# Window attention followed by four experts: reordered loads, junk matmuls in batch 0, and interleaved expert layers

## The chip, the cores and the metric

The kernel runs on one core of a Trainium2 chip. The metric is the device time of one execution, in microseconds (us). Most figures below are medians of several runs. Every run here was of the ordinary, fast state. A profile is one such execution, taken by the hardware profiler; its span is about 1.7 us shorter than the time measured for the same execution.

The array's granted clock is either full or half (1.0 or 0.5) in every record. The first record starts at 42.5 us in the profile before, and for the time before it the profile prints 1.00. Start-to-start distances of matmuls tell the truth there: matmuls of 512 columns at recorded half clock start 0.43 us apart, at full clock 0.22.

## The reference, cut to what matters

```
scores = (q @ k.T) / 8              # 4 batches, 8 heads, 768 positions, 64 wide
keep   = key < 4  or  0 <= query - key < 128
a      = softmax(where(keep, scores, -1e9))
x      = (a @ v), heads side by side          # 3072 tokens x 512
p      = domain_probs / sum(domain_probs)
out    = sum over 4 experts of p[:, e] * (relu(x @ w1[e]) @ w2[e])   # 512 -> 1024 -> 512
```

## The kernel before

Attention goes by batch (four) and by pair of heads (four per batch). A pair transposes q and k on TensorE (trq, trk), copies them out, multiplies scores (spsum), takes exp on ScalarE, multiplies by the mask on VectorE, multiplies by V (opsum), normalises, and transposes back (trx) into xT. This is a serial chain. The names ending in psum, and trq, trk and trx, are buffers in PSUM, the memory that the kernel's matmuls write to. Reading such a buffer out, for hpsum by the relu, is called its eviction; in these programs the next matmuls into it come after that. The experts take tokens in chunks of 512: 8 groups of 4 matmuls (hpsum), relu, then 4 groups of 8 matmuls (mopsum).

The order in the program text is not the order on the engine; it is laid out at compile time. The program has the experts behind all of attention, yet in the trace before an hpsum matmul starts at 32.89 us, within batch 0. So expert matmuls stand among attention's, and in these traces a matmul that waits holds up those behind it (one of them for 2.22 us, below).

The parts that the change touches, cut:

```
# 1. GpSimd builds the masks, then issues every load
nc.gpsimd.memset(MASK, 1.0) ... nc.gpsimd.affine_select(...) x 13
nc.gpsimd.dma_start(out=dp_nat, ...)
# 2. loads of a pair stand inside the pair: 4 for q and k, 2 for v
for hp in range(NHP):
    for ph in range(2): nc.gpsimd.dma_start(out=qn[:, :, ph, :], ...); (same for kn)
    ...
# 3. order of the whole
emit_attention_batch(0); emit_weight_loads(0); emit_weight_loads(1)
emit_attention_batch(1); emit_weight_loads(2); emit_weight_loads(3)
emit_attention_batch(2); emit_attention_batch(3)
# 4. experts
for c in range(NCH):
    for e in range(E):
        for fb in range(NFB):        # 8 groups of 4 hpsum matmuls, two PSUM buffers
            ...; relu -> ht
        for sub in range(NSUB):      # 4 groups of 8 mopsum matmuls
            ...
    nc.sync.dma_start(out=<1 MB of the chunk>, in_=out_sb)
```

The softmax here doesn't subtract the row's maximum and nothing guards it: scores larger than these inputs give would overflow.

Of the kernel before, what the change touches and what calls it, by code (L numbers as in the profile page):

```python
# [9 lines left out]
ALU = mybir.AluOpType  # L10
AX = mybir.AxisListType
FP32 = mybir.dt.float32
BF16 = mybir.dt.bfloat16
# [3 lines left out]
def kernel(  # L17
# [12 lines left out]
    nc = tc.nc  # L30

    B, H, S, D = q.shape
    NSINK = int(n_sink)
    WIN = int(window)
    E, Dm, F = moe_w1.shape
# [28 lines left out]
    def out_contribs(qb):  # L64
# [24 lines left out]
    ps_h = ctx.enter_context(tc.tile_pool(name="ps_h", bufs=2, space=bass.MemoryType.PSUM))  # L89
    ps_o = ctx.enter_context(tc.tile_pool(name="ps_o", bufs=2, space=bass.MemoryType.PSUM))  # L90

    ident = consts.tile([P, P], BF16, name="ident")
    nc.gpsimd.memset(ident, 1.0)
    nc.gpsimd.affine_select(
        out=ident, in_=ident, compare_op=ALU.is_ge, fill=0.0,
        base=0, pattern=[[1, P]], channel_multiplier=-1,
    )
    nc.gpsimd.affine_select(
        out=ident, in_=ident, compare_op=ALU.is_ge, fill=0.0,
        base=0, pattern=[[-1, P]], channel_multiplier=1,  # L100
    )

    MASK = consts.tile([P, AT_W], BF16, name="MASK")
    nc.gpsimd.memset(MASK, 1.0)  # L104

    def sel_diag(cs):
        nc.gpsimd.affine_select(  # L107
            out=MASK[:, cs : cs + P], in_=MASK[:, cs : cs + P],
            compare_op=ALU.is_ge, fill=0.0,
            base=0, pattern=[[1, P]], channel_multiplier=-1,  # L110
        )

    def sel_prev(cs):
        nc.gpsimd.affine_select(  # L114
            out=MASK[:, cs : cs + P], in_=MASK[:, cs : cs + P],
            compare_op=ALU.is_gt, fill=0.0,
            base=0, pattern=[[-1, P]], channel_multiplier=1,
        )

    sel_diag(0)  # L120
    sel_prev(P)
    nc.gpsimd.memset(MASK[:, 2 * P : S], 0.0)
    nc.gpsimd.memset(MASK[0:NSINK, 0:S], 1.0)
    for jb in range(1, NJB):
        cs = JB_ACOL[jb]
        sel_diag(cs)
        if jb < NJB - 1:
            sel_prev(cs + P)

    dp_nat = consts.tile([P, Ntok // P, E], FP32, name="dp_nat")  # L130
    nc.gpsimd.dma_start(  # L131
        out=dp_nat, in_=moe_domain_probs.rearrange("(tb p) e -> p tb e", p=P)
    )
    rowsum = consts.tile([P, Ntok // P], FP32, name="rowsum")
    nc.vector.reduce_sum(out=rowsum, in_=dp_nat, axis=AX.X)
    recip_rs = consts.tile([P, Ntok // P], FP32, name="recip_rs")
    nc.vector.reciprocal(out=recip_rs, in_=rowsum)
    scale_t = consts.tile([P, Ntok // P, E], FP32, name="scale_t")
    nc.vector.tensor_mul(
        scale_t, dp_nat, recip_rs[:, :, None].to_broadcast([P, Ntok // P, E])  # L140
    )

    w1_sb = {}
    w2_sb = {}

    def emit_weight_loads(e):
        for db in range(NDB):
            t = wpool.tile([P, F], BF16, name=f"w1_{e}_{db}", tag=f"w1_{e}_{db}")
            nc.gpsimd.dma_start(out=t, in_=moe_w1[e, db * P : (db + 1) * P, :])
            w1_sb[(e, db)] = t  # L150
        for fb in range(NFB):
            t = wpool.tile([P, Dout], BF16, name=f"w2_{e}_{fb}", tag=f"w2_{e}_{fb}")
            nc.gpsimd.dma_start(out=t, in_=moe_w2[e, fb * P : (fb + 1) * P, :])  # L153
            w2_sb[(e, fb)] = t

    xT = []
    for hp in range(NHP):
        t = xtp.tile([P, Ntok], BF16, name=f"xT_{hp}", tag=f"xT_{hp}")
        xT.append(t)

    def emit_attention_batch(b):
        for hp in range(NHP):
            h0 = 2 * hp
            qn = ap_sb.tile([P, NQB, 2, D], BF16, name="qn", tag="qknat", bufs=8)
            kn = ap_sb.tile([P, NQB, 2, D], BF16, name="kn", tag="qknat", bufs=8)
            for ph in range(2):
                nc.gpsimd.dma_start(  # L167
                    out=qn[:, :, ph, :],
                    in_=q[b, h0 + ph].rearrange("(sb p) d -> p sb d", p=P),
                )  # L170
                nc.gpsimd.dma_start(  # L171
                    out=kn[:, :, ph, :],
                    in_=k[b, h0 + ph].rearrange("(sb p) d -> p sb d", p=P),
                )
            qT = ap_sb.tile([P, S], BF16, name="qT", tag="qkT", bufs=8)
            kT = ap_sb.tile([P, S], BF16, name="kT", tag="qkT", bufs=8)
            trq = ps_mix.tile([P, S], BF16, name="trq", tag="mix")
# [8 lines left out]
            nc.scalar.copy(out=qT, in_=trq)  # L186
            nc.vector.tensor_copy(out=kT, in_=trk)  # L187

            vx = []
            for ph in range(2):  # L190
                vext = ap_sb.tile([P, NJB, 72], BF16, name="vext", tag="vext", bufs=8)
                nc.gpsimd.dma_start(  # L192
                    out=vext[:, :, 0:D],
                    in_=v[b, h0 + ph].rearrange("(jb p) d -> p jb d", p=P),
                )
                nc.gpsimd.memset(vext[:, :, D : D + 1], 1.0)
                vx.append(vext)

            onat = ap_sb.tile([P, NQB, P], BF16, name="onat", tag="onat", bufs=4)

            for ph in range(2):
                pb = ph * 64
                aT = ap_sb.tile([P, AT_W], BF16, name="aT", tag="aT", bufs=4)
                for (cstart, cwidth, mms) in CHUNKS:
                    spsum = ps_mix.tile([P, cwidth], FP32, name="spsum", tag="mix")
                    off = 0
                    for (jb, qoff, ncols) in mms:
                        qs = JB_QSTART[jb] + qoff
                        nc.tensor.matmul(  # L209
                            spsum[:, off : off + ncols],  # L210
                            lhsT=kT[pb : pb + 64, jb * P : (jb + 1) * P],
                            rhs=qT[pb : pb + 64, qs : qs + ncols],
                            start=True,
                            stop=True,
                        )
                        off += ncols
                    nc.scalar.activation(  # L217
                        out=aT[:, cstart : cstart + cwidth],
                        in_=spsum[:, 0:cwidth],
                        func=AF.Exp,  # L220
                        scale=scale,
                    )
                    nc.vector.tensor_mul(  # L223
                        aT[:, cstart : cstart + cwidth],
                        aT[:, cstart : cstart + cwidth],
                        MASK[:, cstart : cstart + cwidth],
                    )

                opsum = ps_aout.tile([P, NQB, 66], FP32, name="opsum", tag="ao")
                for qb in range(NQB):  # L230
                    contribs = out_contribs(qb)
                    for ci, (jb, acol) in enumerate(contribs):
                        nc.tensor.matmul(  # L233
                            opsum[:, qb, 0 : D + 1],
                            lhsT=aT[:, acol : acol + P],
                            rhs=vx[ph][:, jb, 0 : D + 1],
                            start=(ci == 0),
                            stop=(ci == len(contribs) - 1),
                        )
# [5 lines left out]
                    recip[:, :, None].to_broadcast([P, NQB, D]),  # L245
                )

            trx = ps_mix.tile([P, S], BF16, name="trx", tag="mix")
            for qb in range(NQB):
                nc.tensor.transpose(  # L250
# [1 line left out]
                )  # L252
            nc.vector.tensor_copy(out=xT[hp][:, b * S : (b + 1) * S], in_=trx)

    emit_attention_batch(0)
    emit_weight_loads(0)
    emit_weight_loads(1)
    emit_attention_batch(1)
    emit_weight_loads(2)
    emit_weight_loads(3)  # L260
    emit_attention_batch(2)
    emit_attention_batch(3)

    relu_ct = 0
    for c in range(NCH):
        t0 = c * CH
        out_sb = mo_sb.tile([P, NSUB, Dout], FP32, name="out_sb", tag="osb", bufs=2)
        for e in range(E):
            hts = []
            for fb in range(NFB):  # L270
                hpsum = ps_h.tile([P, CH], FP32, name="hpsum", tag="h")
                for db in range(NDB):
# [4 lines left out]
                        start=(db == 0),  # L277
                        stop=(db == NDB - 1),
                    )
                ht = mo_sb.tile([P, CH], BF16, name="ht", tag="hT", bufs=18)  # L280
                relu_ct += 1
                if relu_ct % 3 == 0:
                    nc.vector.tensor_scalar_max(out=ht, in0=hpsum, scalar1=0.0)  # L283
                else:
                    nc.scalar.activation(out=ht, in_=hpsum, func=AF.Relu)  # L285
                hts.append(ht)
            for sub in range(NSUB):
                tb = c * NSUB + sub
                dst = out_sb[:, sub, :]
                opsum = ps_o.tile([P, Dout], FP32, name="mopsum", tag="o")  # L290
                for fb in range(NFB):
                    nc.tensor.matmul(  # L292
                        opsum,
                        lhsT=hts[fb][:, sub * P : (sub + 1) * P],
                        rhs=w2_sb[(e, fb)],
                        start=(fb == 0),
                        stop=(fb == NFB - 1),
                    )
                sc = scale_t[:, tb, e : e + 1]
                if e == 0:  # L300
                    nc.vector.tensor_scalar(  # L301
                        out=dst, in0=opsum, scalar1=sc, scalar2=None, op0=ALU.mult
                    )
                else:
                    nc.vector.scalar_tensor_tensor(  # L305
                        out=dst,
                        in0=opsum,
                        scalar=sc,
                        in1=dst,
                        op0=ALU.mult,  # L310
                        op1=ALU.add,
                    )
        nc.sync.dma_start(
            out=out[t0 : t0 + CH, :].rearrange("(s p) d -> p s d", p=P),
            in_=out_sb,
        )


# [33 lines left out]
```

## Time and profile before

| | before |
|---|---|
| time, median of 16 runs | 462.99 us (460.71 to 465.5) |
| span of the profile | 460.7 us |
| first transpose on TensorE | 14.99 us |
| first pair of batch 1 begins | 59.16 us |
| last matmul ends | 454.63 us |

The page of the kernel before: the busy time of each engine (PE is TensorE's matmuls, PEld its weight loads, DVE VectorE, ACT ScalarE, POOL GpSimd), then two rows of the span in 40 slices (busy tenths of TensorE, and its granted clock in tenths of full speed).

```profile
PE 429.9 (93%) x2528; PEld 207.0 (45%) x2528; DVE 202.3 (44%) x387; ACT 154.0 (33%) x273; POOL 113.8 (25%) x198
...
PE   0568899999999999999999999999999999999994
...
PEclk9999559999999999999999999999999999999999
```

TensorE is at least 90% busy from the sixth slice to the last but one. One slice is 11.5 us, and the two slices marked 5 ran at half clock, so the loose part is the first 70 us. The slices before them are marked 9 because no clock change was recorded before 42.5 us.

The timeline of TensorE in the kernel before: start us, length us, line, operation, out<-in, count, and in brackets the idle time before it and what ended it.

```profile
14.99 0.69 PE L180 MATMUL trq<-ident,qn 128*128 128x128 bf16 x5 [14.99 <-DMA qn<-in_q_dram]
...
26.05 0.31 PE L180 MATMUL trq<-ident,qn 128*128 128x128 bf16 x1
26.16 0.31 PE L183 MATMUL trk<-ident,kn 128*128 128x128 bf16 x1
...
32.89 0.61 PE L273 MATMUL hpsum<-xT,w 128*128 128x512 bf16 x1 [2.22 <-DMA w<-in_moe_w_dram]
```

Three things are to be read here. TensorE did nothing for 15 us. Transposes of 128 columns start 0.107 us apart, as they do later where half clock is recorded (46 to 70 us); they start 0.056 us apart after 72 us, at recorded full clock. And an expert matmul, placed early, held the queue for 2.22 us until its weights landed.

Why 15 us: the timeline of GpSimd (POOL), which issues the loads.

```profile
6.75 0.28 POOL L107 TENSOR_SCALAR_AFFINE_SELECT MASK<-MASK 128x128 bf16<-128x128 bf16 x1
6.99 1.55 POOL L131 DMA_DIRECT2D dp_nat<-in_moe_domain_probs_dram  x1
8.54 0.83 POOL L167 DMA_DIRECT2D qn<-in_q_dram  x1
```

The first load of q is issued only at 8.54 us, behind the masks and a small load that nobody needs yet.

Busy time by stretch. The first four stretches are the four pairs of batch 0, the fifth is the first pair of batch 1. Columns: the stretch and its length, busy us (and instructions) of PE, PEld, DVE, ACT and POOL, then granted clock, DMA share and GB/s.

```profile
15.00:25.80 10.80, 8.38 (x62) 4.96 (x63) 4.89 (x13) 5.04 (x9) 10.80 (x18) 1.00 1.87 119
25.80:39.00 13.20, 9.32 (x67) 5.40 (x65) 5.58 (x14) 4.93 (x9) 9.39 (x19) 1.00 1.40 168
39.00:48.60 9.60, 7.79 (x67) 4.95 (x66) 5.45 (x14) 4.62 (x9) 6.09 (x12) 0.86 1.17 204
48.60:59.20 10.60, 9.09 (x67) 5.26 (x66) 5.45 (x14) 5.04 (x9) 9.87 (x15) 0.50 1.77 147
...
59.10:72.50 13.40, 13.40 (x83) 6.29 (x81) 6.09 (x15) 7.12 (x13) 13.40 (x25) 0.60 1.77 116
```

A warning about the busy column. TensorE is shown busy for 8.38 of 10.8 us in the first pair, but it is slow, not full: at the distances seen at full clock (0.056 us for a transpose, 0.029 for an output matmul, 0.22 for 512 columns) the same matmuls would need less than half of that (an estimate).

The chain of waits in the dense part: start us, length us, what.

```profile
300.64 7.11 PE hpsum L273 x32
307.75 6.91 PE mopsum L292 x32
314.65 7.07 PE hpsum L273 x32
```

32 matmuls of the first layer take 0.16 to 0.20 us more than 32 of the second. Start to start, the last matmul of an hpsum group takes 241 ns on average and all others 215 to 216. After 90 late group ends (219 ns and more, from 200 us on) the next matmul starts 50 to 54 ns after a relu has ended: it waits for the eviction.

### The profile page before, as it was taken

What the parts mean: (1) busy time and instruction counts of PE and PEld (TensorE: products, weight loads), DVE (VectorE), ACT (ScalarE), POOL (GpSimd) and SP (SyncE); (2) the same over time, 40 slices, a digit from 0 to 9 for tenths busy, and PEclk for the clock granted to TensorE, in tenths of its full rate; (3) what the DMA queues carried; (4) which work ended last, traced back from release to release, by engine and by line L of the source; (5) the groups of instructions that cost most, each with busy time, mean ns of one, the idle gap of its engine ahead of it and who ended that gap; (6) DMA issues with size and microseconds to landing.
All of it is one profiled execution on the core that took longest, in us unless ns stands there. A gap on an engine that the chain in (4) does not pass through costs nothing.

```text
span 460.7 us, 6303 instructions
## 1 busy us (share of the span) xinstructions
PE 429.9 (93%) x2528; PEld 207.0 (45%) x2528; DVE 202.3 (44%) x387; ACT 154.0 (33%) x273; POOL 113.8 (25%) x198
## 2 busy tenths in 40 slices
PE   0568899999999999999999999999999999999994
PEld 0344545555555554444444444444444444444441
DVE  0345546867767773333332333233333323333332
ACT  1435455476566752211223211222211232212220
POOL 9985896699940000000000000000000000000000
PEclk9999559999999999999999999999999999999999
DMA  1999999999990002000020000200001000200002
GB/s 7 127 143 204 162 119 172 205 129 119 117 61 1 2 1 91 1 0 0 1 91 1 1 0 1 91 1 1 1 38 53 1 0 1 90 1 1 1 1 91
DMA packets 85437, 24.58 MB, mean 53 GB/s; under 512 B 76144, under 2 KB 80288, under 8 KB 85408
## 3 DMA queue, kind: packets, MB, share of 16 engines
q0 software_dynamic: 82240, 17.88, 43.4%
q1 hardware_dynamic: 3168, 6.29, 3.6%
q8 instruction: 20, 0.33, 0.3%
q14 instruction: 9, 0.07, 0.0%
HBM read 35.70 MB, written 6.29 MB: 91 GB/s over the span
## 4 chain that ended last, share of the span: by engine, by line
PE 90%; POOL 6%; DVE 1%; DMA 1%; issue 0%; ACT 0%; POOLq 0%
PE hpsum L273 38%; PE mopsum L292 37%; PE spsum L209 7%; PE opsum L233 4%; POOL kn L171 1%; PE trx L250 1%; POOL qn L167 1%; POOL vext L192 1%; PE trq L180 1%; PE trk L183 1%; DMA w<-in_moe_w_dram 1%; DVE onat L242 1%; POOL MASK L104 0%; POOL dp_nat L131 0%; POOL MASK L107 0%; POOL MASK L114 0%
## 5 line engine op out<-in xcount | busy, mean ns | idle before, releaser
L273 PE MATMUL hpsum<-xT,w 128*128 128x512 bf16 x768 | 185.8, 383 | 2.2 <-DMA w<-in_moe_w_dram 2.2
L292 PE MATMUL mopsum<-w,ht 128*128 128x512 bf16 x768 | 178.2, 380 | 0.0
L285 ACT ACTIVATE ht<-hpsum 128x512 bf16<-128x512 f32 x128 | 76.5, 597 | 223.0 <-PE hpsum L273 223.0
L273 PEld LDWEIGHTS <-w 128*128 128x128 bf16 x768 | 73.5, 97 | 96.3 <-issue 21.4
L292 PEld LDWEIGHTS <-ht 128*128 128x128 bf16 x768 | 74.0, 98 | 88.5 <-issue 5.7
L305 DVE SCALAR_TENSOR_TENSOR out_sb<-mopsum,scale_t,out_sb 128x512 f32<-128x512 f32 x72 | 54.0, 750 | 74.9 <-PE mopsum L292 74.9
L283 DVE TENSOR_SCALAR ht<-hpsum 128x512 bf16<-128x512 f32 x64 | 44.2, 691 | 87.0 <-PE hpsum L273 86.1
L217 ACT ACTIVATE aT<-spsum 128x512 bf16<-128x512 f32 (+1 forms) x128 | 65.3, 576 | 17.0 <-PE spsum L209 16.3
L223 DVE TENSOR_TENSOR aT<-aT,MASK 128x512 bf16<-128x512 bf16 (+1 forms) x128 | 49.3, 402 | 22.7 <-ACT aT L217 19.9
L209 PE MATMUL spsum<-qT,kT 64*128 64x256 bf16 (+2 forms) x224 | 47.3, 318 | 1.7 <-ACT qT L186 1.6
L233 PEld LDWEIGHTS <-aT 128*128 128x128 bf16 x480 | 25.3, 105 | 17.9 <-DVE aT L223 4.3
L233 PE MATMUL opsum<-vext,aT 128*128 128x65 bf16 x480 | 31.2, 206 | 2.2 <-DVE onat L242 2.0
L186 ACT COPY qT<-trq 128x768 bf16<-128x768 bf16 x16 | 12.8, 799 | 52.8 <-PE trq L180 40.9
L171 POOL DMA_DIRECT2D kn<-in_k_dram x32 | 30.1, 941 | 0.7 <-PE trk L183 0.7
L167 POOL DMA_DIRECT2D qn<-in_q_dram x32 | 29.8, 931 | 1.5 <-PE trk L183 0.8
L192 POOL DMA_DIRECT2D vext<-in_v_dram x32 | 28.9, 948 | 4.3 <-issue 2.7
L180 PE MATMUL trq<-ident,qn 128*128 128x128 bf16 x96 | 15.1, 247 | 15.0 <-DMA qn<-in_q_dram 15.0
L301 DVE TENSOR_SCALAR out_sb<-mopsum,scale_t 128x512 f32<-128x512 f32 x24 | 18.0, 750 | 23.7 <-PE mopsum L292 23.7
L209 PEld LDWEIGHTS <-kT 64*128 64x128 bf16 x224 | 18.3, 101 | 21.6 <-DVE kT L187 9.0
L153 POOL DMA_DIRECT2D w<-in_moe_w_dram x32 | 17.5, 588 | 13.4 <-DMA w<-in_moe_w_dram 12.6
L242 DVE TENSOR_TENSOR onat<-opsum,recip 128x384 bf16<-128x384 f32 x32 | 17.7, 554 | 0.5
L180 PEld LDWEIGHTS <-qn 128*128 128x128 bf16 x96 | 10.6, 113 | 15.0 <-issue 15.0
(26 smaller groups left out, 94.2 us busy)
## 6 DMA issues: line engine op xcount, KB each, us to landing
out_dram<-out_sb SPq DMA_DIRECT2D x6, 1024.0 KB, 4.3
w<-in_moe_w_dram POOLq DMA_DIRECT2D x16, 256.0 KB, 6.3
w<-in_moe_w_dram POOLq DMA_DIRECT2D x32, 128.0 KB, 7.3
qn<-in_q_dram POOLq DMA_DIRECT2D x32, 96.0 KB, 3.8
kn<-in_k_dram POOLq DMA_DIRECT2D x32, 96.0 KB, 3.8
vext<-in_v_dram POOLq DMA_DIRECT2D x32, 96.0 KB, 3.6
dp_nat<-in_moe_domain_probs_dram POOLq DMA_DIRECT2D x1, 48.0 KB, 5.5
```

Source lines behind the costliest of these rows:

```text
L167: nc.gpsimd.dma_start(out=qn[:, :, ph, :], in_=q[b, h0 + ph].rearrange("(sb p) d -> p sb d", p=P),)
L171: nc.gpsimd.dma_start(out=kn[:, :, ph, :], in_=k[b, h0 + ph].rearrange("(sb p) d -> p sb d", p=P),)
L192: nc.gpsimd.dma_start(out=vext[:, :, 0:D], in_=v[b, h0 + ph].rearrange("(jb p) d -> p jb d", p=P),)
L209: nc.tensor.matmul(spsum[:, off : off + ncols], lhsT=kT[pb : pb + 64, jb * P : (jb + 1) * P], rhs=qT[pb : pb + 64, qs : qs + ncols], start ...
L217: nc.scalar.activation(out=aT[:, cstart : cstart + cwidth], in_=spsum[:, 0:cwidth], func=AF.Exp, scale=scale,)
L223: nc.vector.tensor_mul(aT[:, cstart : cstart + cwidth], aT[:, cstart : cstart + cwidth], MASK[:, cstart : cstart + cwidth],)
L233: nc.tensor.matmul(opsum[:, qb, 0 : D + 1], lhsT=aT[:, acol : acol + P], rhs=vx[ph][:, jb, 0 : D + 1], start=(ci == 0), stop=(ci == len(co ...
L273: nc.tensor.matmul(hpsum, lhsT=w1_sb[(e, db)][:, fb * P : (fb + 1) * P], rhs=xT[db][:, t0 : t0 + CH], start=(db == 0), stop=(db == NDB - 1),)
L283: nc.vector.tensor_scalar_max(out=ht, in0=hpsum, scalar1=0.0)
L285: nc.scalar.activation(out=ht, in_=hpsum, func=AF.Relu)
L292: nc.tensor.matmul(opsum, lhsT=hts[fb][:, sub * P : (sub + 1) * P], rhs=w2_sb[(e, fb)], start=(fb == 0), stop=(fb == NFB - 1),)
L305: nc.vector.scalar_tensor_tensor(out=dst, in0=opsum, scalar=sc, in1=dst, op0=ALU.mult, op1=ALU.add,)
```

## The change

Its intent: start the chain of batch 0 sooner, keep the array at full clock through it with matmuls whose result is thrown away ("junk"), and hide the eviction of hpsum. The core of the diff:

```diff
+    junk = consts.tile([P, 512], BF16, name="junk")
+    nc.vector.memset(junk, 0.25)
+    junk_ps = ps_o.tile([P, 512], FP32, name="junk_ps", tag="o")
+    def warm(lhsT, rhs, n): ...            # n matmuls into junk_ps
+    warm(junk[:, 0:P], junk, 18)           # at the start
-    nc.gpsimd.dma_start(out=dp_nat, ...)
+    nc.sync.dma_start(out=dp_nat, ...)
     ...
+    first_loads[(0, 0)] = emit_loads(0, 0) # first pair's loads, then the masks
+    ident, MASK: memsets now on nc.vector, affine_selects on nc.gpsimd
     ...
     def emit_attention_batch(b):
         for hp in range(NHP):
+            if b == 0 and hp == 2: emit_w1_load(0)
             ...                            # V of both heads in one load
+            if b == 0:
+                for cs in (0, 512, 1024):
+                    for t in aTs:
+                        warm(t[:, cs : cs + P], t[:, cs : cs + 512], 2)
     ...
     emit_attention_batch(0)
     emit_weight_loads(0)                   # w2 of an expert in one load
+    first_loads[(1, 0)] = emit_loads(1, 0); first_loads[(1, 1)] = emit_loads(1, 1)
     emit_weight_loads(1)                   # (the same for batch 2)
     ...
+                (ht has 20 buffers instead of 18)
                 hts.append(ht)
+                if fb % 2 == 1 and pending_mm2:
+                    pending_mm2.pop(0)()   # second layer of the expert before
             for sub in range(NSUB):
+                pending_mm2.append(make_mm2(c, e, sub, hts, out_sb))
-        nc.sync.dma_start(out=<1 MB of the chunk>, in_=out_sb)
+                (inside make_mm2, e == 3)   nc.sync.dma_start(out=<256 KB of sub>, in_=dst)
```

## The prediction

> **What bounds it now.** TensorE. From 72 us to the end its matmuls are back to back (stretches table: 10.0 of 10 us busy). One 512-column matmul every 216 ns is the floor there; only the last matmul of each hpsum group takes 239 ns, 192 times (4.5 us in all), which I read as a wait for one of the two hpsum buffers to be evicted. So nothing is gained on VectorE, ScalarE or GpSimd as such; the time to win is before 72 us and after the last matmul (454.6 us; span 460.7).
>
> The front, from the timeline: GpSimd first builds the masks (to 7.0 us) and issues dp_nat (to 8.5), so the first transpose waits until 15.0. The four head pairs of batch 0 then take 10.7, 13.1 (2.2 of it an hpsum matmul that waits for a weight DMA), 9.7 and 10.6 us, to 59.2. Within a pair there is a serial chain: transposes, copies, scores, exp, mask, output, normalise, transpose. TensorE is also slow there: transposes start 107 ns apart, against 56 ns after 72 us; output matmuls about 55 against 29. [...]granted clock 0.50 from 50 to 70 us, full after; the 1.0 recorded before 40 us contradicts the 107 ns and is not to be believed.
>
> **The change.** (a) Loads first, masks later, merged V and w2 issues. GpSimd starts at 0.8 us; the second qn issue ends near 3.2, and before it took 4.0 us from there to the first transpose: about 7.2 instead of 15.0. Gain 7.8. (b) 18 junk matmuls fill the wait for that load ([...]free), and 12 per pair (2.6 us warm, 10.4 in all) fill gaps of batch 0, to keep the clock. A warm pair, estimated from the partly warm third pair (9.7) less the cold transposes and the cold last output group, is 8.3 us of chain with 3.6 of TensorE work; junk fits mostly, costing perhaps 0.7. So four pairs take 36 us: batch 0 ends near 43 instead of 59.2. (c) 59 to 70 us, now at half clock, becomes warm: 5.4 us. (d) Interleaving second-layer matmuls with the first-layer ones hides the hpsum eviction: up to 4.5, say 3. (e) The final store is 256 KB instead of 1 MB: 1 to 2 us off the tail. Weights and batch 1 loads should land before they are needed; GpSimd issues less.
>
> **Sum.** Batch 0 to 43.3; then 1528 expert matmuls x 216.4 ns = 330.7; 12 pairs at 4.55 us (what the dense region before paid, switching included) = 54.6; leftover waits 1.5; tail 4.3: span 434.4. Median was 2.2 over the span: **437 us**, range 429 to 446. Faster by over 2%: 0.95; within: 0.04; slower: 0.01.
>
> **What would show it.** First real transpose at 7 to 8 us; transposes of batch 0 56 ns apart; its pairs 8.5 to 9.5 us each; batch 1 begins at 41 to 46; no clock near 0.5 after 8 us; hpsum group ends at 216 ns; TensorE dense from batch 1 on; last matmul to end about 4.3 us.
>
> **What would make it wrong.** The compile-time order puts junk or hpsum matmuls ahead of chain work, and TensorE, in order, waits behind them; junk is too thin and the clock falls back (pairs 10.6 us, total 444); the 16-byte dp_nat packets delay the first q and k; weights late after batch 0; the next pair's transposes overlap the chain (better: 430).

## The result, and the profile after

| | before | after |
|---|---|---|
| time, median | 462.99 us (16 runs) | 438.12 us (11 runs, 436.21 to 439.52) |
| span of the profile | 460.7 | 437.4 |
| first transpose | 14.99 | 7.93 |
| the four pairs of batch 0, start to start | 10.9, 13.2, 9.6, 10.6 | 8.5, 12.4, 8.5, 8.5 |
| batch 1 begins | 59.16 | 45.77 |
| last matmul ends | 454.63 | 433.21 |
| from there to the end | 6.04 | 4.17 |

The ratio of the times is 0.9463 (95% interval 0.9439 to 0.9487). Ratios here are the mean time of one kernel's fast runs over that of the other's of the same rounds, so they are not quite the ratios of the quoted medians. A twelfth run of the changed kernel, of 440.89 us, is not counted there; with it the median would be 438.15.

The page of the kernel after:

```profile
PE 427.1 (98%) x2594; PEld 206.9 (47%) x2594; DVE 206.1 (47%) x392; ACT 152.8 (35%) x273; POOL 85.5 (20%) x133
...
PE   7899999999999999999999999999999999999996
...
PEclk9979999999999999999999999999999999999999
```

The empty front is gone. One slice is still marked with a reduced clock, the third (22 to 33 us).

TensorE's timeline after:

```profile
1.52 6.57 PE L100 MATMUL junk_ps<-junk 128*128 128x512 bf16 x18 [1.52 <-DVE junk L95]
7.93 0.22 PE L172 MATMUL trq<-ident,qn 128*128 128x128 bf16 x1
7.98 0.22 PE L175 MATMUL trk<-ident,kn 128*128 128x128 bf16 x1
...
18.64 0.60 PE L348 MATMUL hpsum<-xT,w 128*128 128x512 bf16 x2 [1.40 <-DMA w<-in_moe_w_dram]
```

The transposes start 0.05 to 0.06 us apart from the first on. But an hpsum matmul waits for weights again, in the second pair. The stretches after, again four pairs of batch 0 and the first of batch 1:

```profile
7.90:16.40 8.50, 7.28 (x75) 4.40 (x74) 5.02 (x13) 4.82 (x9) 8.50 (x17) 1.00 1.21 84
16.40:28.80 12.40, 10.75 (x80) 5.33 (x77) 5.59 (x14) 4.93 (x9) 10.59 (x15) 0.72 1.90 166
28.80:37.30 8.50, 7.85 (x81) 4.53 (x78) 5.58 (x14) 4.82 (x9) 4.80 (x7) 1.00 1.70 169
37.30:45.80 8.50, 7.85 (x80) 4.53 (x78) 5.58 (x14) 4.81 (x9) 6.83 (x11) 1.00 2.08 174
...
45.70:54.90 9.20, 8.94 (x86) 4.87 (x84) 6.05 (x15) 6.82 (x13) 4.57 (x7) 1.00 1.26 183
```

The second pair stands out: 12.4 us at a mean clock of 0.72. The first pair of batch 1, with 83 matmuls in 13.4 us before, now has 86 in 9.2 us, at a mean granted clock of 1.00 instead of 0.60.

The chain of waits in the dense part after:

```profile
300.25 1.73 PE mopsum L316 x8
301.98 1.73 PE hpsum L348 x8
303.71 1.73 PE mopsum L316 x8
```

Eight matmuls of either layer now take the same time; every one starts 216 ns after the one before.

The span fell by 23.3 us. Along the time axis that is 13.4 to the start of batch 1 (59.16 to 45.77), 8.0 from there to the last matmul (395.5 to 387.4), and 1.9 after it.

### The profile page after: what moved, and what is told of

It reads as the page before. It is cut to its first block, busy times and chain, and to the rows that moved or that the text cites. A ratio compares the mean times of both kernels' runs of the same rounds, so it can differ in the third digit from the quotient of the medians.

```text
span 437.4 us, 6407 instructions
## 1 busy us (share of the span) xinstructions
PE 427.1 (98%) x2594; PEld 206.9 (47%) x2594; DVE 206.1 (47%) x392; ACT 152.8 (35%) x273; POOL 85.5 (20%) x133
## 4 chain that ended last, share of the span: by engine, by line
PE 93%; POOL 3%; DMA 1%; ACT 1%; DVE 0%; issue 0%; POOLq 0%
PE mopsum L316 39%; PE hpsum L348 38%; PE spsum L193 7%; PE opsum L217 3%; PE junk_ps L100 2%; DMA w<-in_moe_w_dram 1%; PE trx L239 1%; PE trq L172 1%; PE trk L175 1%; POOL qn L141 1%; POOL kn L145 1%; ACT qT L178 1%; POOL vx L150 0%; ACT aT L201 0%; POOL MASK L260 0%
## 5 line engine op out<-in xcount | busy, mean ns | idle before, releaser
L348 PE MATMUL hpsum<-xT,w 128*128 128x512 bf16 x768 | 190.1, 379 | 1.4 <-DMA w<-in_moe_w_dram 1.4
L316 PE MATMUL mopsum<-w,ht 128*128 128x512 bf16 x768 | 187.7, 379 | 0.0
L193 PE MATMUL spsum<-qT,kT 64*128 64x256 bf16 (+2 forms) x224 | 41.0, 284 | 2.7 <-ACT qT L178 1.6
L141 POOL DMA_DIRECT2D qn<-in_q_dram x32 | 27.3, 854 | 20.4 <-DMA w<-in_moe_w_dram 19.0
L217 PEld LDWEIGHTS <-aT 128*128 128x128 bf16 x480 | 24.9, 99 | 13.3 <-DVE aT L207 2.3
L217 PE MATMUL opsum<-vx,aT 128*128 128x65 bf16 x480 | 28.7, 196 | 0.4
L145 POOL DMA_DIRECT2D kn<-in_k_dram x32 | 27.2, 851 | 3.0 <-PE opsum L217 1.4
L150 POOL DMA_DIRECT2D vx<-in_v_dram x16 | 16.6, 1041 | 2.8 <-DMA w<-in_moe_w_dram 2.7
L100 PE MATMUL junk_ps<-aT 128*128 128x512 bf16 x48 | 15.2, 416 | 0.0
L172 PE MATMUL trq<-ident,qn 128*128 128x128 bf16 x96 | 12.4, 219 | 0.0
L175 PE MATMUL trk<-ident,kn 128*128 128x128 bf16 x96 | 12.4, 219 | 0.0
```

The costliest lines, as they stand in the source:

```text
L100: nc.tensor.matmul(junk_ps[:, 0 : rhs.shape[-1]], lhsT=lhsT, rhs=rhs, start=True, stop=True,)
L141: nc.gpsimd.dma_start(out=qn[:, :, ph, :], in_=q[b, h0 + ph].rearrange("(sb p) d -> p sb d", p=P),)
L145: nc.gpsimd.dma_start(out=kn[:, :, ph, :], in_=k[b, h0 + ph].rearrange("(sb p) d -> p sb d", p=P),)
L193: nc.tensor.matmul(spsum[:, off : off + ncols], lhsT=kT[pb : pb + 64, jb * P : (jb + 1) * P], rhs=qT[pb : pb + 64, qs : qs + ncols], start ...
L217: nc.tensor.matmul(opsum[:, qb, 0 : D + 1], lhsT=aT[:, acol : acol + P], rhs=vx[:, ph, jb, 0 : D + 1], start=(ci == 0), stop=(ci == len(co ...
L316: nc.tensor.matmul(opsum, lhsT=hts[fb][:, sub * P : (sub + 1) * P], rhs=w2_sb[e][:, fb, :], start=(fb == 0), stop=(fb == NFB - 1),)
```

## The experiments

All results were correct. Each run timed its kernel beside the kernel before on the same chip. For comparison with the changed kernel I give the median, and the ratio to the kernel before where a difference is small. The starting theory was that the gain is the sum of four things: earlier loads, full clock, hidden eviction, short last store. The main rival was that the junk is mere filler, since batch 0 is a serial chain over other engines.

### Without any junk

```diff
-    warm(junk[:, 0:P], junk, 18)        (and junk, junk_ps)
-            if b == 0: ... warm(t[...], t[...], 2)
```

> After the change, with both kinds of junk matmuls taken out and nothing else. Clock theory: without them the array stays at half clock through batch 0 (transposes 107 ns apart, pairs near 10.6 us instead of 8.5) and some 10 us into batch 1, as before the change; batch 1 begins near 50 to 52 us instead of 45.8, and the time is 446 to 450 us (438.1 with junk). Rival, early loads alone: batch 0 is bound by a serial chain over ScalarE and VectorE, the junk is filler, and the time stays 436 to 439.

Measured: 446.8 us. The pairs took 11.1, 9.6, 9.6 and 10.6 us and batch 1 began at 47.9 us. Its first pair:

```profile
47.80:61.20 13.40, 13.40 (x84) 6.33 (x83) 6.09 (x15) 7.14 (x13) 8.01 (x13) 0.60 1.86 178
```

So the junk is worth 8.7 us between medians, and the rival falls. But the time was not where I expected most of it. In the profiles batch 0 ends only 2.1 us later without junk; another 4.2 us is lost in the first pair of batch 1 (13.4 us against 9.2), at a mean clock of 0.60 against 1.00. Together these are the 6.3 us between the two profiles; the profiled run was the fastest of the four without junk. That batch 0 loses so little is partly because the changed kernel has a bad second pair of its own: against a later variant without that fault (a_fill below, batch 1 at 43.1 us) batch 0 ends 4.8 us later.

### Only the start burst, and only the junk in the pairs

```diff
a_startonly:  -  if b == 0: ... warm(t[...], t[...], 2)
a_pairsonly:  -  warm(junk[:, 0:P], junk, 18)
```

> After the change with the 18 junk matmuls at the start kept and the 12 per pair taken out. Clock theory: the first pair runs at full clock (8.5 us or less), but TensorE is only busy about 40% within a pair, so the clock falls back in the second pair and stays low until batch 1: 444 to 448 us. Rival, the start burst alone is enough: 436 to 439.

> After the change with the 18 junk matmuls at the start taken out and the 12 per pair kept. Clock theory: the first pair begins at half clock (107 ns transposes) and its own junk, twice as long then, delays it, so it takes 11 to 12 us; the junk releases the clock by the second pair. Cost 2 to 4 us against the changed kernel: 440 to 442. If the per-pair junk is worth nothing: near the kernel without any junk.

Measured: 445.3 us with the start burst alone, as expected, and 439.1 with the pair junk alone, less than the 440 to 442 expected. The clock of the burst was lost during the first pair (recorded fall at 14.2 us). The junk in the pairs does nearly all of the work. With pair junk alone the first pair took 13.3 us instead of 8.5, and the first transpose could start at 6.95 us, a microsecond earlier than behind the burst. TensorE's timeline shows that only this one could:

```profile
6.95 0.27 PE L169 MATMUL trq<-ident,qn 128*128 128x128 bf16 x1 [6.95 <-POOL MASK L264]
7.69 0.27 PE L172 MATMUL trk<-ident,kn 128*128 128x128 bf16 x1 [0.47 <-DMA kn<-in_k_dram]
```

The second one waits for k, and the twelfth starts at 8.71 us, against 8.54 behind the burst. Yet batch 1 began at 45.69 us, as in the changed kernel (45.77): there the second pair gives back what the burst won. The ratios are 0.9514 and 0.9463 with overlapping intervals, so the worth of the burst, 1 us between medians and 2.4 by the ratios, is not resolved.

### Without interleaving, and interleaving alone

```diff
a_nointer:  -                if fb % 2 == 1 and pending_mm2: pending_mm2.pop(0)()
            -                pending_mm2.append(make_mm2(...))
            +                make_mm2(c, e, sub, hts, out_sb)()
b_inter:    the kernel before, with the interleaved expert loop (1 MB stores kept)
```

> After the change with the second-layer matmuls of an expert put back straight behind its first-layer ones. Buffer theory: the last matmul of each hpsum group takes 239 ns again instead of 216 in the dense part, about 23 ns for some 160 to 190 groups, so 4 to 5 us more: 442 to 443. Rival, interleaving did nothing: 438.

> The kernel before with only the interleaving of second-layer matmuls added (1 MB stores kept). Buffer theory: last matmuls of hpsum groups 216 instead of 241 ns in the dense part, 25 ns x 192 = 4.8 us at most: 458 to 459 us against 462.9. The kernel after without interleaving lost 8.8, of which its group ends at 255 ns explain about 7: so the interleaving should give less here than it costs there.

Measured: 446.9 us without it, a loss of 8.8, where 4 to 5 had been expected; and 459.4 us for interleaving alone, ratio 0.9937 (0.9897 to 0.9978), a gain of 2.9 (1.0 to 4.8). The chain of waits without interleaving shows the loss:

```profile
299.93 7.21 PE hpsum L348 x32
307.14 6.91 PE mopsum L316 x32
314.05 7.25 PE hpsum L348 x32
```

In the dense part the last matmul of an hpsum group takes 255 ns on average there, 241 in the kernel before, and 216 wherever the layers are interleaved. 39 ns for 192 groups would be 7.5 us, and 25 ns is 4.8 us (estimates). (The ends of groups 1 and 8 of each eight take 215 to 216 ns; only the six between are late.) The profile shows 6.0 us: from the start of batch 1 to the last matmul this kernel takes 393.5 us, the changed one 387.4. The other 2.0 us between the two profiles lie in the front, where the second pair took 14.6 us instead of 12.4, with a wait of 2.40 instead of 1.40 us for weights; whether that is chance, one profile of each does not show. Nor is it shown why a group end takes 255 ns here and 241 in the kernel before. Interleaving alone gave less than the 4.8 us at stake. In its profile the group ends are at 216 ns as promised, but the early weight wait was 3.61 us instead of 2.22 and no rise of the clock was recorded before 64.8 us; batch 1 began 2.1 us later. These losses do not explain the small gain of the runs, though. That profile is of the fastest of its four runs and is 4.8 us shorter than the profile before (455.9 against 460.7). From batch 1 to the last matmul it gained 6.8 us, 3 of them in the first pair of batch 1, where the clock rose earlier in the pair. So why the full form was worth more than the same form added alone stays open.

### One store of 1 MB per chunk

```diff
-            if e == E - 1:
+            if e == E - 1 and sub == NSUB - 1:      # and the whole chunk in one store
```

> After the change with one store of 1 MB per chunk instead of four of 256 KB. Tail theory: from the last matmul to the end 6.0 us again instead of 4.2, so 1.5 to 2 us more: 439.7 to 440.2. Rival, stores are not on the path: 438.

Measured: 441.1 us, 3.0 above the changed kernel and about 1 above what was expected. Its profile shows 6.04 us from the last matmul to the end against 4.17, which is 1.9 us; the remainder is within the spread of runs. The lists of DMA issues, first of this kernel, then of the changed one (KB each, median us to landing):

```profile
out_dram<-out_sb SPq DMA_DIRECT2D x6, 1024.0 KB, 4.3
```

```profile
out_dram<-out_sb SPq DMA_DIRECT2D x24, 256.0 KB, 2.0
```

Only the last store is on the path, so only its length counts: at its end the kernel before waits 3.5 us for a store of 1 MB, the changed one 1.6 us for one of 256 KB. These stores are issued by SyncE.

### Masks first again

```diff
-    first_loads[(0, 0)] = emit_loads(0, 0)     (before ident and MASK)
-    nc.vector.memset(ident/MASK, ...)
+    nc.gpsimd.memset(ident/MASK, ...)
+    first_loads[(0, 0)] = emit_loads(0, 0)     (after them)
```

> After the change with the masks and the identity built on GpSimd ahead of the first loads again. Early-load theory: everything of batch 0 shifts by the 6 to 7 us that GpSimd is busy with the masks; the 18 junk matmuls end at 7.7 us and their warmth is lost by then, so the first pair also runs cold: batch 1 begins at 52 to 54 us instead of 45.8, 444 to 447 us. Rival, the clock and not the loads made the gain: 438 to 440.

Measured: 444.1 us, 6.0 more. From TensorE's timeline:

```profile
12.64 0.69 PE L172 MATMUL trq<-ident,qn 128*128 128x128 bf16 x5 [5.17 <-DMA qn<-in_q_dram]
```

The first transpose is 4.7 us later, and the full clock that the burst had brought is lost in the 5.17 us of waiting (recorded fall at 12.2 us). Batch 1 begins at 51.5 us, 5.7 later; so most of the loss is there before the clock comes into it. So the early loads are a cause of their own, and the rival that the clock alone made the gain falls.

### Why does the second pair of batch 0 take 12.4 us?

The two hpsum matmuls that wait in it were my suspect. In a first trial the junk output was moved into both buffers of the hpsum pool, which keeps every hpsum matmul out of batch 0:

```diff
-    junk_ps = ps_o.tile([P, 512], FP32, name="junk_ps", tag="o")
+    junk_ps = [ps_h.tile([P, 512], FP32, name=f"junk_ps{i}", tag="h") for i in range(2)]
```

> After the change, with the junk output moved from the pool of the second layer to both buffers of the first layer's pool, so that no hpsum matmul can be placed before the end of batch 0; nothing else. In the changed kernel the second pair took 12.4 us against 8.5 for the other three: two hpsum matmuls stand before its score matmuls and wait for w1 (1.4 us), and the clock then drops for 6.8 us. If that wait is the cause, the second pair takes 8.4 to 9 us, no clock drop, batch 1 begins near 42 us instead of 45.8, and with 8 matmuls (1.7 us) left for later the time is 434.5 to 437 against 438.1. Rival, the pair's own loads came late or the clock falls by itself: the second pair stays at 12 us and the time at 438 or more.

Measured: 441.4 us, slower. The wait was gone, but the second pair still took 11.6 us, and the fourth now took 10.0. My suspect was at most an accomplice. The timeline and the stretches of this kernel:

```profile
17.17 0.22 PE L175 MATMUL trk<-ident,kn 128*128 128x128 bf16 x1
18.22 0.81 PE L193 MATMUL spsum<-qT,kT 64*128 64x512 bf16 x5 [0.83 <-ACT qT L178]
19.28 0.32 PE L193 MATMUL spsum<-qT,kT 64*128 64x256 bf16 x2 [0.25 <-ACT aT L201]
```

```profile
17.20:20.60 3.40, 2.18 (x18) 1.12 (x15) 1.89 (x5) 2.77 (x6) 2.80 (x4) 1.00 1.08 187
20.60:24.00 3.40, 3.40 (x24) 1.60 (x21) 2.23 (x8) 2.06 (x4) 2.01 (x3) 0.50 1.92 169
```

The same two stretches of the changed kernel, where the wait for weights falls into the first:

```profile
16.90:20.30 3.40, 1.75 (x15) 0.81 (x13) 0.89 (x3) 1.50 (x3) 3.10 (x5) 1.00 1.07 186
20.30:23.70 3.40, 3.40 (x22) 1.47 (x21) 1.95 (x5) 2.46 (x5) 1.89 (x3) 0.50 1.85 165
```

Without the wait the clock fell all the same, at 20.6 us, with no idle gap longer than 0.83 us: at the head of a pair TensorE waits for the copies (0.83 us) and for the first exp (0.25 us). All clock records here last a multiple of 3.413 us (1, 7 and 114 times in the profile before, 4, 2 and 120 times in the one after), save the last of each trace, which the end cuts off. So I cut the first 75 us of the first ten profiles into windows of that length, laid by the records, and added up for each the time in which columns stream (columns over clock; 512 columns take 0.22 us at full clock and 0.43 at half). The window from 17.2 us has a share of 0.41, that of the changed kernel from 16.9 us 0.38. With the last four profiles added, the whole count is:

| clock in the window, then in the next | windows | streaming share |
|---|---|---|
| full, then half | 17 | 0.00 to 0.57 (15 of them 0.53 or less) |
| full, then full | 187 | 0.55 to 1.00 |
| half, then full | 31 | 0.75 to 1.00 (28 of them 0.88 or more) |
| half, then half | 72 | 0.00 to 0.96 |

The shares are an estimate, worked out from the columns and starts of the matmuls in the traces: they count transposes and 64-row matmuls like any other and take the clock before the first record as half. In the profiles before and after no matmul is missing (2528 and 2594 records). In the 14 profiles, then, the 17 falls followed shares of 0.57 or less, and the 187 windows that full clock outlasted had 0.55 or more; the two ranges hardly overlap. The 31 rises followed 0.75 or more, but eight windows of 0.88 or more did not bring the rise, so there the shares separate less well. Other counts: weighting each matmul by its active rows separates the falls as well. Leaving transposes out does not: 31 windows that kept full clock then lie at or below the highest share before a fall, against 4 with them. By what the clock is set was not shown; these are counts of what went together. The first record lay at 5.2 to 7.4 us in the profiles of kernels with the burst, so the windows lie differently from one to the next. Whether the lull at the head of a pair falls into one window or is split by two would then be chance (an estimate, not tested).

Four more junk matmuls, in the lull itself, test this. They read xT of the pair before, so they become ready just there:

```diff
+            if b == 0 and hp > 0:
+                warm(xT[hp - 1][:, 0:P], xT[hp - 1][:, 0:512], 4)
             nc.scalar.copy(out=qT, in_=trq)
```

> After the change with four more junk matmuls in each of pairs 2 to 4 of batch 0, fed from xT of the pair before, so that they fall into the lull between the transposes and the first scores. Lull theory, formed after the first eight runs: the clock falls after any 3.41 us window in which TensorE streams less than about half of the time, and the window over the start of the second pair had 0.38 to 0.47. Four matmuls add 0.86 us, or 0.25 of a window: no fall after 7 us, second pair 8.5 to 9.5 us instead of 12.4, batch 1 begins at 42 to 43.5 us, 435 to 436.5 us against 438.1. Rival, the fall has another cause: clock falls near 20 us all the same and the time is 438 to 440.

Measured: 437.0 us, a little over the 435 to 436.5 expected, ratio 0.9451 (0.9417 to 0.9485). From TensorE's timeline:

```profile
17.10 1.04 PE L100 MATMUL junk_ps<-xT 128*128 128x512 bf16 x4
18.07 0.82 PE L195 MATMUL spsum<-qT,kT 64*128 64x512 bf16 x5
```

In its profile no fall of the clock was recorded until the end of the kernel, the second pair took 8.9 us and batch 1 began at 43.1 us. The third pair then took 9.3 us because its k landed late (a wait of 0.58 us). So the lull theory holds in the trace. Its runs fit, too: the mean recorded clock was 0.996 or more in five of six, and in 2 of 12 runs of the changed kernel (time before the first record counts as full there). The time went only part of the way that it promised, and the ratio cannot be told from the 0.9463 of the changed kernel.

The wait was also taken away without removing the two matmuls, by loading their weight tile ahead of the second pair; alone, with fill, and with fill but no start burst:

```diff
a_w1split:             +  if b == 0 and hp == 1: emit_w1_load(0, [0])
a_w1split_fill:        +  the same, and warm(xT[hp - 1]..., 2)
a_w1split_fill_pairs:  -  the same as a_w1split_fill, without warm(junk..., 18)
```

> After the change with the first of the four w1 tiles of expert 0 loaded ahead of the second pair's own loads, so that the two hpsum matmuls in front of the scores find their weights. Wait theory: the 1.4 us wait goes; with the two matmuls in the lull the window has about 0.5 of streaming, at the edge, so the clock may or may not fall: 434 to 438 us, second pair 8.5 us if it stays and 11 if not.[...]

> Both: the early w1 tile and two junk matmuls more in the lull of pairs 2 to 4. Lull theory: no wait and no fall of the clock, four pairs of 8.5 us, batch 1 begins at 42 us, 434 to 435 us; the fastest so far. Rival: the loads of the second pair, later by one weight tile, stall it: 436 to 439.

> The same without the 18 junk matmuls at the start. Before, the start burst was worth only 1 us (439.1 without, 438.1 with), since the second pair gave its 4.8 us back. If that account is right, here the burst is worth its full 4 to 5 us: 438.5 to 440. Rival, the burst never matters because later pairs wait for loads anyway: within 1 us of the kernel with it.

Measured: 437.4 (435.75 to 441.39), 437.7 (435.89 to 438.68) and 439.1 us. The first has the widest spread of all these kernels. Its slowest run was the profiled one, with three recorded falls of the clock before 46 us. Its two fastest, 435.75 and 436.30, had a mean recorded clock of 1.00 (time before the first record counts as full there). With fill, one fall was left in the profile, in the first pair, which has no fill (share 0.47). The kernel with both the early tile and fill missed its 434 to 435 us. The last lay in its range, 438.5 to 440, but the difference that the range stood for missed: the burst was worth 1.5 us between medians here too, not 4 to 5, and the intervals of the two ratios overlap (0.9416 to 0.9484 and 0.9458 to 0.9518). So the account that the second pair's wait alone hides the burst's worth is not borne out; with the burst the first pair can still fall, as in the profile of a_w1split_fill at 12.2 us.

No variant beat the changed kernel beyond the noise: 436.96, 437.38 and 437.66 us against 438.12, with ratios 0.945 to 0.946 against 0.946. Not tested on their own were the merged loads of V and w2, the earlier load of w1, and the loads issued ahead for batches 1 and 2.

## Why the prediction was right

The time of 438.1 us lay 1 us from the predicted 437. Term by term, against the profile of the changed kernel:

| term of the sum | predicted | measured |
|---|---|---|
| first transpose | 7.2 | 7.93 |
| four pairs of batch 0 | 36 (8.3 of chain plus 0.7 each) | 37.8 (three of 8.5, one of 12.4) |
| start of batch 1 to the last matmul | 330.7 + 54.6 + 1.5 = 386.8 | 387.4 |
| last matmul to the end | 4.3 | 4.2 |
| span | 434.4 | 437.4 |

- "About 7.2 instead of 15.0": nearly. The second qn had landed at 6.85 us, but the last matmul of the burst starts only at 7.7 us. The prediction counted to the second q load; every other transpose needs the second k load, which landed at 7.61 us. So the junk delayed the first transpose by a microsecond and the last of the twelve not at all (8.54 us with the burst, 8.71 without): it was nearly free, as predicted. The cause, masks ahead of loads, was confirmed: masks first cost 6.0 us.
- "To keep the clock": right in kind, as taking the junk out cost 8.7 us. "No clock near 0.5 after 8 us" was wrong: it was half from 20.3 to 27.1 us, and "junk is too thin and the clock falls back" stood among the things that could go wrong. The prediction gave no measure of how thick junk has to be; the windows above give one for these profiles, the streaming share (0.57 or less before every fall). Three pairs took 8.5 us, 0.5 less than the 9.0 allowed for, and one 3.4 more; these misses partly cancel.
- A placed-ahead hpsum matmul waiting for weights was also foreseen as a risk, and came: 1.40 us. The sum held no room for it.
- "59 to 70 us, now at half clock, becomes warm: 5.4": measured 4.2 between the first pairs of batch 1.
- "Hides the hpsum eviction: up to 4.5, say 3": the group ends are at 216 ns, so all of it (25 ns a group) was hidden in the dense part. What it is worth was put too low: without it the profile is 6.0 us longer from batch 1 to the last matmul.
- "1 to 2 us off the tail": 1.9.
- "Weights and batch 1 loads should land before they are needed": TensorE is dense from batch 1 on, as predicted.

The span was 3 us over the sum, 2.5 of it in the front. The median came nearer than that because the profiled execution, at 439.1 us, was slower than the median, and because I had added 2.2 us to a span instead of 1.7. So part of the closeness is luck.

## What to carry to other kernels

Filling gaps of a latency-bound stretch with junk matmuls paid twice here: in the stretch itself (2.1 us, or 4.8 once the heads of pairs 2 to 4 were filled as well) and in the dense stretch right behind it, which then starts at full clock (4.2 us). Look for the thinnest window of a few microseconds, not for the longest gap: here the clock fell after 3.4 us with a streaming share of 0.41 and no gap over 0.83 us. Where one engine builds constants and also issues the first loads, issue the loads first (6.0 us here). Interleave two matmul layers so that one layer's PSUM eviction falls behind the other's matmuls (group ends of 216 ns here instead of 241 and 255), but measure in place: taking a part out of the full change and adding it alone gave 8.8 and 2.9 us here, and why is open.
